# Two more planner gates on ScalarE copies in a kernel of a 2-D Fourier filter and a two-layer MLP

## The chip, the cores and the metric

The kernel runs on one core of a Trainium2 chip. The metric is the device time of one execution in microseconds (us); before the change the median of three runs is 149.49 us, from 149.27 to 149.67. TensorE (PE) multiplies matrices into PSUM, which has eight banks of 512 fp32 columns on 128 partitions. ScalarE (ACT) and VectorE (DVE) copy and compute on what lies in PSUM and in SBUF, GpSimd (POOL) and SyncE (SP) mostly issue DMAs here. Each engine works through its own instructions in order, and semaphores tie the engines together. In the profile, PEld is the weight load that goes ahead of a matmul.

## The reference

`x` is 2048 x 640, the hidden width is 1536, and all inputs are bf16.

```python
def _A_ref(x, w_r, w_i):
    X = jnp.fft.rfft2(x.astype(jnp.float32), axes=(-2, -1))
    X = X * (w_r + 1j * w_i)
    return jnp.fft.irfft2(X, s=(S, D), axes=(-2, -1)).astype(jnp.bfloat16)

def _B_ref(x, w1, b1, w2, b2):
    h = _gelu(jnp.einsum("bsd,df->bsf", x, w1) + b1)
    return jnp.einsum("bsf,fd->bsd", h, w2) + b2

xn = _layernorm(x, axis=-1)
return x + _A_ref(xn, A_w_r, A_w_i) + _B_ref(xn, B_w1, B_b1, B_w2, B_b2)
```

So each output row is the row of x, plus the filtered row, plus the row of the MLP, in which the vector b2 is the same for every row.

## The kernel before

**Tiles and stages.** The 2048 rows are 16 tiles of 128. Each is normalised (L667, DVE) and turned into `xnT`, the first eight tiles on PE, the last eight by transposing DMAs. The Fourier transforms are matmuls with tables. The forward one goes through PE groups that the code calls aps (one for each pair of tiles: ten matmuls of 128 columns with `gtab`; the DVE folds of L702 and L706 make their input, and a copy at L718 takes the 1280 columns of a pair out of PSUM into `XV`), bps, and cps; DVE multiplies by the filter (L833, L837); dps starts the way back, and after it sixteen transposing DMAs (L858, on SP) fill `XV` anew. The last part is the inverse transform of the rows, by the six `GROUPS` of two or three tiles, and then one closing matmul for each tile with `htab`, which goes into the same bank as the second MLP layer, is added to x + b2 by DVE (L950), and leaves for HBM.

**The MLP.** The first layer runs in five `BLOCKS` of 4, 2, 2, 4 and 4 tiles. In each block there are twelve hidden chunks; a chunk is five matmuls (for a block of four tiles, 512 columns each) into one bank, `hps`, and one activation on ScalarE (L760) that empties the bank into `gT`. The fourth block (number 3 in the code) is tiles 8 to 11. Its banks come from banks 4 to 7. The second layer of the tiles in `KEEP` is done early, in the middle of the kernel; its result sits in a pair of the same banks 4 to 7 (`kps`) until DVE adds it to x + b2 (L941). While such a pair is held, the block has two banks, and the third chunk of a block needs the bank of the first one back.

**b2's rows.** For each tile ScalarE writes the row b2 as fp32 to all 128 partitions (L917, 640 columns), into memory that the input x or `xnT` no longer needs; then a DMA from POOL (L935) adds x to it in place. Tile 11's row goes to the end of `X`, and needs the normalisation of all sixteen tiles to be done. The row has priority 5, the lowest of ScalarE's work.

**The inverse groups.** For each group, 8 or 12 matmuls with 128 rows and as many with 32 rows (with `getab`) write four banks (`eps`), of the banks 0 to 3. The 32-row ones read a remainder of `XV`; for groups 1 to 5 (`NEAR`) that remainder is first copied, 128 columns a tile, into `W1` (the remainder copies, L878, buffers xr1 to xr5, by ScalarE or DVE). All five can start when the last transposing DMA has landed. Two copies (L885, buffer yo), one for each half of the columns, then take the group out of PSUM; these are the inverse copies. DVE folds them twice (L889, L894) for the closing matmul.

**The planner.** Nothing of this order is written out by hand except where a gate says so. Every piece of work is a `K.op` with the engines that may do it and a cost for each, a priority, and what it reads and writes. `schedule` (L223) is a greedy list scheduler with its own clock: it always places the work that can start first; among what can start within 0.03 us of that on an engine, the highest priority goes first, and work that two engines may do goes to the one that would end it first. The order that comes out is the order of the instructions on each engine. `deps` (from reads, writes and `after`) become semaphore waits in `sync`. A `gate` does not: it only makes the planner place a piece no earlier, on its clock, than the start of the piece that it names. The costs that the change touches are these:

```python
def mm_us(n):
    return max(n / 2400.0 + 0.0027, 0.0265)
def dve_us(n, rate=1.0):
    return 0.066 + n / 960.0 / rate
def act_us(n, ptr=0):
    return 0.067 + n / 1200.0 + 0.078 * ptr
```

Of the kernel before, what the change touches and what calls it, by code (L numbers as in the profile page):

```python
# [9 lines left out]
ACT = mybir.ActivationFunctionType  # L10
# [3 lines left out]
D = 640  # L14
# [76 lines left out]
# [10 lines that stand above are left out]
# [78 lines left out]
class Sched:  # L179
# [190 lines left out]
    def emit(self, es, last):  # L370
# [54 lines left out]
CP = (((0, 1, ((0, 1, ["dve"]),)), (1, 3, ((1, 3, ["dve"]),)), (3, 5, ((3, 5, ["act"]),))), ((0, 2, ((0, 2, ["dve"]),)), (2, 5, ((2, 5, ["dve", "act"]),))),  # L425
      ((0, 2, ((0, 2, ["dve"]),)), (2, 5, ((2, 5, ["act", "dve"]),))), ((0, 2, ((0, 2, ["dve"]),)), (2, 5, ((2, 5, ["act", "dve"]),))))
NEAR = (1, 2, 3, 4, 5)
RP = 1.0
EARLY = 3
FIRST = ([(j, (c,), 0, 6) for c, j in ((0, 0), (0, 1), (0, 2), (1, 0), (1, 1), (1, 2), (0, 3), (1, 3))] + [(4, (0, 1), 0, 6)]  # L430
# [3 lines left out]
def bass_parallel_sum__spectral_gfnet__dense_activation_gelu__prompt_kernel(  # L434
# [20 lines left out]
    K = Sched(nc, ["sp", "pe", "act", "dve", "pool"])  # L455
    with ExitStack() as es:
        def sb(name, shape, dtype=BF):
            return es.enter_context(nc.sbuf_tensor(name, shape, dtype))

        def view(t, off, dims):  # L460
            width = int(np.prod(t.shape[1:]))
            return bass.AP(tensor=t, offset=off, ap=[[width, 128]] + dims)
# [15 lines left out]
        b2bc = sb("b2bc", [128, D])  # L478
# [23 lines left out]
        def psb(slot, dims, off=0, p0=0, n=128):  # L502
            return bass.AP(tensor=PS, offset=p0 * 4096 + slot * 512 + off, ap=[[4096, n]] + dims)
# [15 lines left out]
        def pe(segs, prio, lst, **kw):  # L519

            return K.op([("pe", sum(u for _, u in segs))], prio, mms(lst), alts=[segs], **kw)

        def copy(dst, src, scale=1.0):
            def f(e, name):
                if name == "act":
                    return e.activation(dst(), src(), ACT.Copy, scale=scale)  # L526
                return e.tensor_copy(dst(), src())  # L527
            return f
# [12 lines left out]
        for k in range(12):  # L541
# [3 lines left out]
             reads=[B_warm], writes=[B_id])  # L545
# [7 lines left out]
        B_b1, B_b2b, B_bz = Buf("b1t"), Buf("b2"), Buf("b1z")  # L553
# [76 lines left out]
        for c0, n in [(c, 1) for c in range(4)] + [(c, 2) for c in range(4, 16, 2)]:  # L630
            pr = 100 - c0 / 2
            B_mv, B_r = Buf("mv"), Buf("r")
            for c in range(c0, c0 + n):
                B_st = Buf("st")
                for h in range(2):
                    o = K.op([("dve", 0.393)], pr, lambda e, _, c=c, h=h: e.bn_stats(stats[:, c, 6 * h:6 * h + 6], view(X, c * D + H2 * h, [[1, H2]])),  # L636
                         reads=[B_x[c]], writes=[B_st], gate=mv_ops[:1])
# [4 lines left out]
                 reads=[B_mv, B_mh], writes=[B_r] + B_rs[a:b])  # L642

        for pair in range(8):
# [10 lines left out]
            for n in range(2):  # L655
                c = 2 * pair + n
                pr = 100 - c / 2
                cuts = [(0, 1), (1, 5)] if not c else [(0, 5)]
                B_xn = {}
                for j0, j1 in cuts:  # L660
# [4 lines left out]
                    if c == 0 and j0:  # L665
# [3 lines left out]
                        reads=[B_x[c], B_rs[c]], writes=[xn, b], gate=mv_ops[1:2] if c or j0 else [])  # L669
# [5 lines left out]
                if c in BYDMA:  # L675
                    ring_ops.append(K.op([("sp", 1.3)], 500, lambda e, _, c=c, n=n, xnv=xnv: e.dma_start_transpose(xnT[:, c, :, :], xnv(n, 0, [[1, D]])),
                         reads=[B_xn[0], xn], writes=[B_xnT[c]], rows=(40, 256)))
# [4 lines left out]
                for j0, j1, parts in CP[c] if c < 4 else ((0, 5, ((0, 5, ["dve", "act"]),)),):  # L682
# [11 lines left out]
                    for a, b, engs in parts:  # L694
# [4 lines left out]
                             reads=[tps], writes=[B_xnT[c]] if c > 3 else [B_xnT[c]] + [B_xnj[c, j] for j in range(a, b)])  # L699
            pr = 100 - pair - FOLD[pair]  # L700
# [3 lines left out]
            for k, op in enumerate((ALU.add, ALU.subtract)):  # L704
                for o_, o0, o1, w in ((128 * k, 0, H2 - 1, 128), (512 + 32 * k, 128, H2 - 129, 32)):
                    ring_ops.append(K.op([("dve", dve_us(4 * w, 2))], pr, lambda e, _, op=op, x1v=x1v, xfv=xfv, o_=o_, o0=o0, o1=o1, w=w: e.tensor_tensor(  # L706
                        out=xfv(o_, [[D, 2], [2 * w, 2], [1, w]]), in0=x1v(o0, [[D, 2], [H2, 2], [1, w]]), in1=x1v(o1, [[D, 2], [H2, 2], [-1, w]]), op=op),
                        reads=[x1], writes=[xf]))
            aps = Buf(f"aps{pair}", psum, 3, ZONE["aps"])
            for n in range(2):  # L710
                c = 2 * pair + n
                o = pe([("128", 5 * mm_us(128))], pr, lambda c=c, n=n, xfv=xfv, aps=aps: [
                    (psb(aps.slot, [[4, 64], [1, 2]], 256 * j + 2 * n), xfv(n * D + 128 * j, [[1, 128]]), gtab[:, 128 * c:128 * c + 128], True, True) for j in range(5)],
                    reads=[xf, B_g], writes=[aps])
                ring_ops.append(o)
                a_ops.append(o)
            for js in [[int(j) for j in g] for g in XASPLIT[pair].split()]:
# [3 lines left out]
                     reads=[aps], writes=[B_xa[pair]])  # L721

        B_gT = {}
        l1_ops, l1_of = [], {}
        h0 = [Buf(f"h0_{k}", psum, 1, ZONE["h0"]) for k in range(6)]
        first = {}

# [17 lines left out]
        for bi, (c0, nt) in enumerate(BLOCKS):  # L745
            for fc in range(NFC):
                hps = Buf(f"hps{bi}_{fc}", psum, 1, ZONE["hps"] if bi else ZONE["h1"]) if bi or fc > 5 else h0[fc]
                bg = Buf(f"gT{bi}_{fc}")
                for c in range(c0, c0 + nt):
                    B_gT[c, fc] = bg  # L750
                pr = PRIO["hps"] - bi - fc / 20
                part_ = []
                if bi or fc > 5:
                    for js in ((0, 1, 2), (3, 4)):
                        part_ = [pe([("128", len(js) * mm_us(128 * nt))], pr + 0.01 * len(part_), lambda c0=c0, nt=nt, fc=fc, hps=hps, js=js: [
                            (psb(hps.slot, [[1, 128 * nt]]), view(W1, F * j + 128 * fc, [[1, 128]]), xnT[:, c0:c0 + nt, j, :], j == 0, j == 4) for j in js],
                            reads=[B_w1s[fc // 6, j] for j in js] + B_xnT[c0:c0 + nt], writes=[hps], gate=part_)]
                        l1_ops += part_
                        l1_of.setdefault(bi, []).extend(part_)
                g_op = K.op([("act", act_us(128 * nt, 1))], pr + PRIO["gelu"] + GP[bi], lambda e, _, c0=c0, nt=nt, fc=fc, hps=hps: e.activation(  # L760
                    gT[:, fc, 128 * c0:128 * (c0 + nt)], psb(hps.slot, [[1, 128 * nt]]), ACT.Gelu_apprx_tanh, bias=b1col[:, fc:fc + 1], scale=1.0),
                    reads=[hps, B_b1c], writes=[bg])
                if not bi and fc == GATE0:
                    a_ops[0].gate.append(g_op)
                    a_ops[1].gate.append(g_op)
# [14 lines left out]
        def five_segs(n, t):  # L780
            return [("128", 4 * n * mm_us(Q4)), ("32", t)]

        pb_ops, filt_ops, d_ops, v_ops = [], [], [], []
        B_v = [Buf(f"v{q}") for q in range(16)]
        B_xb = {}
        xb_at = {}
        for gi, (c0, n) in enumerate(GROUPS):
# [4 lines left out]
                reads=B_xa + [B_e], writes=[bps, xb]))  # L792
# [8 lines left out]
        for P in range(4):  # L801
# [4 lines left out]
            for r in range(2):  # L806
# [6 lines left out]
                    reads=in_xb + [B_xbpad, B_m], writes=[cps])  # L813
# [16 lines left out]
            for pair, Y, TB, Z in zip(two, Ys, TBs, Zs):  # L830
                pr = PRIO["filt"] - pair / 5
                for k in range(2):
                    filt_ops.append(K.op([("dve", dve_us(4 * KP, 2))], pr, lambda e, _, k=k, Y=Y, TB=TB, pair=pair: e.tensor_tensor(  # L833
                        out=view(TT, TB.slot * 8 * KP + k * 4 * KP, [[2 * KP, 2], [KP, 2], [1, KP]]), in0=yv(Y, k == 1), in1=wv(pair, k), op=ALU.mult),
                        reads=[Y, B_wpad] + (B_w if pair == 7 else [B_w[k]]), writes=[TB], after=ring_ops))
# [4 lines left out]
            for v in range(2):  # L840
# [7 lines left out]
                for pp, U in enumerate(Us):  # L848
                    def evac(e, name, U=U, v=v, uv=uv, dps=dps, pp=pp):
                        for o_, w in ((0, 128), (512, 32)):  # L850
# [3 lines left out]
                         reads=[dps], writes=[U, B_us[pp]], after=a_ops + ring_ops)  # L854
# [13 lines left out]
            return [fin_ops[k[-AHEAD]]] if len(k) >= AHEAD else [l1_ops[-1]]  # L868
        B_yf = {}
        yf_at = {}  # L870
        for gi, (c0, n) in enumerate(GROUPS):
            yo, y2, yf = Buf(f"yo{gi}", p_yo), Buf(f"y2{gi}", p_y2), Buf(f"yf{gi}", p_yf)
            pr = PRIO["eps"] - c0 / 10
            eps_ = Buf(f"eps{gi}", psum, 4, ZONE["eps"])
            near = gi in NEAR
            B_xr = Buf(f"xr{gi}")
            if near:
                K.op([("act", act_us(128 * n)), ("dve", dve_us(128 * n))], pr + RP, copy(  # L878
                    lambda c0=c0, n=n: view(W1, REM + 128 * c0, [[128, n], [1, 128]]), lambda c0=c0, n=n: view(XV, 2048 * 4 + c0, [[1, n], [16, 128]])),
                     reads=B_v, writes=[B_xr], after=l1_ops)  # L880
            pe(five_segs(n, 0.071 * n + (0.014 if near else 0.059)), pr, lambda c0=c0, n=n, eps_=eps_, near=near: five(
                eps_.slot, n, lambda i, g, p0, k: part(W1, p0, k, REM + 128 * (c0 + i), [[1, 128]]) if near and g == 4 else part(XV, p0, k, 2048 * g + c0 + i, [[16, 128]]), getab),
                reads=B_v + [B_ge] + ([B_xr] if near else []), writes=[eps_], gate=[fin_ops[c0 - 5]] if c0 > 8 else [])
            for v in range(2):
                K.op([("act", act_us(320 * n)), ("dve", dve_us(320 * n))], pr,  # L885
                     copy(lambda v=v, yo=yo, n=n: view(Wf, YO + yo.slot * 3 * D + H2 * v, [[D, n], [Q4, 2], [1, Q4]]),
                          lambda v=v, eps_=eps_, n=n: psb(eps_.slot + 2 * v, [[Q4, n], [512, 2], [1, Q4]])), reads=[eps_], writes=[yo], after=filt_ops)
            for k, op in enumerate((ALU.add, ALU.subtract)):
                K.op([("dve", dve_us(320 * n, 2))], pr + 2, lambda e, _, k=k, op=op, yo=yo, y2=y2, n=n: e.tensor_tensor(  # L889
                    out=view(Wf, Y2 + y2.slot * 3 * D + (H2 - 1) * k, [[H2, 2 * n], [1 - 2 * k, Q4]]),  # L890
                    in0=view(Wf, YO + yo.slot * 3 * D, [[H2, 2 * n], [1, Q4]]), in1=view(Wf, YO + yo.slot * 3 * D + Q4, [[H2, 2 * n], [1, Q4]]), op=op),
                    reads=[yo], writes=[y2])
            for k, op in enumerate((ALU.add, ALU.subtract)):
# [3 lines left out]
                    reads=[y2], writes=[yf])  # L897
            for i in range(n):
                c = c0 + i
                kept = c in KEEP  # L900
                xo, os_ = Buf(f"xo{c}"), Buf(f"os{c}", p_os)
                if c in HOME:
                    ki = HOME.index(c)
                    free = [o for j, (t0, nt) in enumerate(BLOCKS) if t0 < 2 * ki + 2 for o in l1_of[j]]

                    def xov(o0, w, ki=ki):
                        return xnT[:].rearrange("p c j t -> p (c j t)").bitcast(F32)[:, D * ki + o0:D * ki + o0 + w]
                else:
                    ki = [b for b in range(16) if b not in HOME].index(c)
                    free = norm_ops[:2 * ki + 2]  # L910
# [3 lines left out]

                xb2 = Buf(f"xz{c}")
                if True:
                    K.op([("act", act_us(D))], 5, lambda e, _, xov=xov: e.activation(xov(0, D), b2bc[:], ACT.Copy), reads=[B_b2b], writes=[xb2], after=free, late=30.0)  # L917

                def sums(o0, w):

# [4 lines left out]
                def second(c, fps, o0, w, pr, gate, base=base):  # L925
                    part_ = []
                    for f0 in range(0, NFC, 3):
# [6 lines left out]
                pr = PRIO["fin"] - c / 10  # L934
                xo_ops[c] = K.op([("pool", 0.9)], 51 - c / 20, lambda e, _, c=c, xov=xov: e.dma_start(xov(0, D), xv[:, c, :], accum_op=ALU.add),  # L935
                     reads=[xb2], writes=[xo], rows=(8, "acc"))
# [6 lines left out]
                for o0, w in [(0, D)] if c < 15 else [(0, H2), (H2, Q4), (H2 + Q4, Q4)]:  # L943
# [5 lines left out]
                        reads=[yf, B_h], writes=[fps, B_f], gate=part_ + ([l1_ops[-1]] if kept else []))  # L949
# [4 lines left out]
                                     reads=[os_, B_o], rows=(8, w * 2 if w * 2 in ROW_NS else 1280)))  # L954
# [38 lines left out]
```

## Time and profile before

| | before |
|---|---|
| time, median of three runs | 149.49 us (149.27 to 149.67) |
| the profiled execution: time | 149.6 us |
| the profiled execution: span | 147.8 us |
| PE busy | 143.7 us, 97% of the span |
| DVE busy | 113.1 us, 77% |
| ACT busy | 83.7 us, 57% |
| POOL busy | 23.0 us, 16% |
| granted TensorE clock, mean | 1.000 |

The span goes from the first to the last instruction; the 1.8 us more of the time lie around it. Matmuls, copies and loads are issued by helpers, so their rows carry the helpers' lines: L515 every matmul, L526 a copy on ScalarE, L527 a copy on DVE, L510 a plain load. A line of the timeline gives start and duration in us, engine, source line, operation, output and input, form, and how many like instructions were merged (x); in brackets, how long the engine had been idle before and what ended that. A merged line's duration goes from the first start to the last end, and successive instructions of one engine overlap in part, so the start of the next line can lie before the end of this one. A matmul's end is modelled, and a matmul that waits for nothing starts before the one ahead of it has ended. A table of windows gives, for each stretch, the busy time of each engine and the number of instructions.

### The profile page before, as it was taken

Reading aid. Unit: us, or ns where it says so; the run is one execution under the profiler, and the core shown is the slowest. Engines: PE = TensorE matmul, PEld = TensorE weight load, DVE = VectorE, ACT = ScalarE, POOL = GpSimd, SP = SyncE. Lnnn points to the kernel's source line nnn. Section 1 sums busy time; section 2 is a strip of 40 time slices with the busy share of each in tenths; the row PEclk is TensorE's granted clock in tenths of the full one; section 3 lists DMA queues with packets and bytes.
Section 4 is the critical chain, followed back from the end, with each engine's and each line's share of the span. In section 5 each row is a group of like instructions: output and inputs, shape, how many; then the busy total and the mean of one; then the engine's idle time right before and its main releaser. Section 6 shows DMA issues by size and latency. Waiting matters only on the chain.

```text
span 147.8 us, 4165 instructions
## 1 busy us (share of the span) xinstructions
PE 143.7 (97%) x1754; PEld 89.5 (61%) x1754; DVE 113.1 (77%) x239; ACT 83.7 (57%) x143; POOL 23.0 (16%) x50
## 2 busy tenths in 40 slices
PE   7999999999999999999999999999999999999993
PEld 7889568898645554656455455334456666566572
DVE  2968999999999254979655796496206999999991
ACT  3123997899998875442878273697757324010300
POOL 4320111420000299600000000000006300000000
PEclk9999999999999999999999999999999999999999
DMA  4999999999688979994015206515453941232233
GB/s 127 291 315 401 360 246 232 362 209 118 122 151 155 239 176 256 268 267 111 0 32 114 40 4 120 60 23 117 84 117 72 225 131 44 99 129 89 89 135 92
DMA packets 28995, 23.00 MB, mean 156 GB/s; under 512 B 17840, under 2 KB 25776, under 8 KB 28848
## 3 DMA queue, kind: packets, MB, share of 16 engines
q1 hardware_dynamic: 26640, 17.48, 47.6%
q0 software_dynamic: 2336, 5.25, 15.5%
q8 instruction: 14, 0.23, 0.6%
q14 instruction: 5, 0.04, 0.1%
HBM read 13.54 MB, written 2.62 MB: 109 GB/s over the span
## 4 chain that ended last, share of the span: by engine, by line
PE 75%; ACT 12%; DMA 5%; SPq 4%; DVE 1%; issue 1%
PE ps L515 74%; ACT gT L760 4%; DMA W<-in_B_w_dram 4%; ACT X L917 3%; SPq L510 2%; SPq L858 2%; DMA XV<-U 2%; ACT xnT L917 2%; ACT W L526 2%; PE ps L687 1%; ACT XV L526 1%; DVE xnT L941 1%; ACT Wf L526 0%; DVE Wf L889 0%; DVE W L950 0%
## 5 line engine op out<-in xcount | busy, mean ns | idle before, releaser
L515 PE MATMUL ps<-W,gT 128*128 128x512 bf16 (+3 forms) x396 | 57.8, 295 | 0.1
L515 PE MATMUL ps<-xnT,W 128*128 128x512 bf16 (+2 forms) x384 | 57.4, 300 | 0.3
L515 PEld LDWEIGHTS ps<-W,gT 128*128 128x128 bf16 x396 | 29.9, 98 | 23.1 <-issue 1.9
L515 PEld LDWEIGHTS ps<-xnT,W 128*128 128x128 bf16 x384 | 31.6, 98 | 18.2 <-issue 2.0
L760 ACT ACTIVATE gT<-ps,b1col 128x512 bf16<-128x512 f32 (+1 forms) x60 | 35.1, 618 | 5.5 <-PE ps L515 4.6
L935 POOL DMA_DIRECT2D xnT<-in_A_x_dram x8 | 9.9, 2787 | 50.5 <-DMA XV<-U 50.5
L526 ACT ACTIVATE Wf<-ps 128x960 bf16<-128x960 f32 (+1 forms) x8 | 6.7, 867 | 17.9 <-PE ps L515 17.9
L636 DVE BATCH_NORM_STATS2 stats<-X 128x6 f32<-128x320 bf16 x32 | 13.7, 465 | 2.0 <-DMA X<-in_A_x_dram 2.0
L526 ACT ACTIVATE Xb<-ps 128x960 bf16<-128x960 f32 (+1 forms) x8 | 9.0, 1166 | 6.9 <-PE ps L515 6.8
L833 DVE TENSOR_TENSOR T<-Y,Wf 128x1288 bf16<-128x1288 bf16 x16 | 12.4, 823 | 0.0
L526 ACT ACTIVATE Y<-ps 128x644 bf16<-128x644 f32 x9 | 6.3, 707 | 7.5 <-PE ps L515 7.5
L935 POOL DMA_DIRECT2D X<-in_A_x_dram x8 | 7.2, 2076 | 20.3 <-DMA Wf<-in_A_w_i_dram 20.3
L941 DVE TENSOR_TENSOR X<-ps,X 128x640 f32<-128x640 f32 x8 | 6.6, 820 | 5.0 <-PE ps L515 5.0
L641 POOL TENSOR_TENSOR rstd<-mv,mhalf 128x2 f32<-128x2 f32 (+1 forms) x10 | 6.6, 663 | 21.0 <-DVE mv L639 21.0
L706 DVE TENSOR_TENSOR T<-T 128x512 bf16<-128x512 bf16 (+1 forms) x32 | 8.3, 314 | 0.1
L527 DVE CAST Xb<-ps 128x640 bf16<-128x640 f32 (+1 forms) x4 | 4.3, 1066 | 5.1 <-PE ps L515 5.1
L950 DVE TENSOR_TENSOR W<-ps,xnT 128x640 bf16<-128x640 f32 (+2 forms) x10 | 6.9, 685 | 1.1 <-PE ps L515 1.0
L527 DVE CAST Y<-ps 128x644 bf16<-128x644 f32 x7 | 5.8, 822 | 2.5 <-PE ps L515 2.5
L837 DVE TENSOR_TENSOR Z<-T 128x644 bf16<-128x644 bf16 x16 | 7.0, 486 | 0.8 <-PE ps L515 0.8
L526 ACT ACTIVATE XV<-ps 128x256 bf16<-128x256 f32 (+4 forms) x9 | 6.7, 750 | 1.3 <-PE ps L515 1.3
L889 DVE TENSOR_TENSOR Wf<-Wf 128x960 bf16<-128x960 bf16 (+1 forms) x12 | 6.8, 594 | 0.6 <-ACT Wf L526 0.6
L515 PE MATMUL ps<-etab,XV 32*128 32x160 bf16 (+1 forms) x128 | 7.2, 232 | 0.0
(59 smaller groups left out, 145.9 us busy)
## 6 DMA issues: line engine op xcount, KB each, us to landing
X<-in_A_x_dram POOLq DMA_DIRECT2D x8, 320.0 KB, 6.8
xnT<-in_A_x_dram POOLq DMA_DIRECT2D x8, 320.0 KB, 9.2
out_dram<-W SPq DMA_DIRECT2D x15, 160.0 KB, 1.8
X<-in_A_x_dram SPq DMA_DIRECT2D x6, 320.0 KB, 7.9
W<-in_B_w_dram SPq DMA_DIRECT2D x4, 480.0 KB, 10.4
W<-in_B_w_dram SPq DMA_DIRECT2D x6, 192.0 KB, 3.9
Wf<-in_A_w_r_dram SPq DMA_DIRECT2D x7, 160.5 KB, 9.4
Wf<-in_A_w_i_dram SPq DMA_DIRECT2D x7, 160.5 KB, 9.5
```

The lines of the kernel that those rows point to most:

```text
L515: ins = e.matmul(o_, lhsT=lw, rhs=rh, start=st, stop=sp_, skip_group_check=True)
L526: return e.activation(dst(), src(), ACT.Copy, scale=scale)
L527: return e.tensor_copy(dst(), src())
L636: o = K.op([("dve", 0.393)], pr, lambda e, _, c=c, h=h: e.bn_stats(stats[:, c, 6 * h:6 * h + 6], view(X, c * D + H2 * h, [[1, H2]])), read ...
L706: ring_ops.append(K.op([("dve", dve_us(4 * w, 2))], pr, lambda e, _, op=op, x1v=x1v, xfv=xfv, o_=o_, o0=o0, o1=o1, w=w: e.tensor_tensor(ou ...
L760: g_op = K.op([("act", act_us(128 * nt, 1))], pr + PRIO["gelu"] + GP[bi], lambda e, _, c0=c0, nt=nt, fc=fc, hps=hps: e.activation(gT[:, fc ...
L833: filt_ops.append(K.op([("dve", dve_us(4 * KP, 2))], pr, lambda e, _, k=k, Y=Y, TB=TB, pair=pair: e.tensor_tensor(out=view(TT, TB.slot * 8 ...
L837: K.op([("dve", dve_us(2 * KP, 2))], pr, lambda e, _, TB=TB, Z=Z, r=r, op=op: e.tensor_tensor(out=view(Zb, Z.slot * 4 * KP + r * KP, [[2 * ...
L917: K.op([("act", act_us(D))], 5, lambda e, _, xov=xov: e.activation(xov(0, D), b2bc[:], ACT.Copy), reads=[B_b2b], writes=[xb2], after=free, ...
L935: xo_ops[c] = K.op([("pool", 0.9)], 51 - c / 20, lambda e, _, c=c, xov=xov: e.dma_start(xov(0, D), xv[:, c, :], accum_op=ALU.add), reads=[ ...
L941: kept_ops.append(K.op([("dve", dve_us(D))], 30, lambda e, _, kps=kps, xov=xov: e.tensor_tensor(out=xov(0, D), in0=psb(kps.slot, [[1, D]]) ...
L950: K.op([("dve", dve_us(w))], 95, lambda e, _, os_=os_, fps=fps, o0=o0, w=w, xov=xov, base=base: e.tensor_tensor(out=view(W1, OST + os_.slo ...
```

## The change

Two gates are added. The second activation of the fourth block (`g31[1]`; `g31` collects the activations of block 3) becomes the gate of tile 11's b2 row. The two inverse copies of group 0 (`yo_ops`) become the gate of the remainder copy of group 5, which is the last of the five. No piece of work is added or removed.

```diff
 NEAR = (1, 2, 3, 4, 5)
+NEARG = 5
+LATEXZ = (11,)
+GX = 1
...
-        l1_ops, l1_of = [], {}
+        l1_ops, l1_of, g31 = [], {}, []
...
                     reads=[hps, B_b1c], writes=[bg])
+                if bi == 3:
+                    g31.append(g_op)
...
         yf_at = {}
+        yo_ops = []
         for gi, (c0, n) in enumerate(GROUPS):
...
-                     reads=B_v, writes=[B_xr], after=l1_ops)
+                     reads=B_v, writes=[B_xr], after=l1_ops, gate=yo_ops if gi >= NEARG else [])
...
             for v in range(2):
-                K.op([("act", act_us(320 * n)), ("dve", dve_us(320 * n))], pr,
+                yo1 = K.op([("act", act_us(320 * n)), ("dve", dve_us(320 * n))], pr,
...
+                if not gi:
+                    yo_ops.append(yo1)
...
                 xb2 = Buf(f"xz{c}")
                 if True:
-                    K.op([("act", act_us(D))], 5, lambda e, _, xov=xov: e.activation(xov(0, D), b2bc[:], ACT.Copy), reads=[B_b2b], writes=[xb2], after=free, late=30.0)
+                    K.op([("act", act_us(D))], 5, lambda e, _, xov=xov: e.activation(xov(0, D), b2bc[:], ACT.Copy), reads=[B_b2b], writes=[xb2], after=free, late=30.0, gate=[g31[GX]] if c in LATEXZ else [])
```

## The prediction

> **What bounds the kernel.** I read the engines' shares first, then the chain of waits, then a table of windows over the parts of the span, then the timelines of the two places that the change touches.
>
> ```profile
> span 147.8 us, 4165 instructions
> PE 143.7 (97%) x1754; PEld 89.5 (61%) x1754; DVE 113.1 (77%) x239; ACT 83.7 (57%) x143; POOL 23.0 (16%) x50
> PE 75%; ACT 12%; DMA 5%; SPq 4%; DVE 1%; issue 1%
> ...
> 42.00:44.00 2.00, 1.88 (x10) 0.68 (x9) 1.97 (x6) 2.00 (x4) 0.00 (x0) 1.00 1.02 169
> 44.00:112.00 68.00, 68.00 (x980) 34.81 (x979) 42.66 (x74) 43.36 (x72) 10.81 (x12) 1.00 0.57 121
> 112.00:118.00 6.00, 5.86 (x68) 3.82 (x66) 5.54 (x9) 3.72 (x5) 3.58 (x4) 1.00 0.74 159
> 118.00:145.00 27.00, 27.00 (x265) 17.35 (x264) 25.98 (x41) 5.07 (x6) 0.00 (x0) 1.00 0.31 100
> ```
>
> PE is the bound. From 42 us on its first column of busy time equals the window, except in two windows, and these are where the two pieces lie that the change moves. So a stall taken out there should come out at the end, unless PE meets it again, and nothing else that moves can gain anything.
>
> **First place: the third chunk of the fourth block.**
>
> ```profile
> 41.06 3.26 PE L515 MATMUL ps<-xnT,W 128*128 128x512 bf16 x13
> 44.16 0.72 PE L515 MATMUL ps<-gtab,T 128*128 128x128 bf16 x10
> 46.31 0.72 PE L515 MATMUL ps<-gtab,T 128*128 128x128 bf16 x10
> 46.86 1.89 PE L515 MATMUL ps<-xnT,W 128*128 128x512 bf16 x8
> 48.59 0.72 PE L515 MATMUL ps<-gtab,T 128*128 128x128 bf16 x10
> ...
> 43.50 0.33 PEld L515 LDWEIGHTS ps<-xnT,W 128*128 128x128 bf16 x3 [0.61 <-ACT gT L760]
> ...
> 41.40 0.85 ACT L917 ACTIVATE xnT<-b2bc 128x640 f32<-128x640 bf16 x1
> 42.02 0.85 ACT L917 ACTIVATE X<-b2bc 128x640 f32<-128x640 bf16 x1
> 42.65 0.80 ACT L760 ACTIVATE gT<-ps,b1col 128x512 bf16<-128x512 f32 x1
> 43.42 0.69 ACT L760 ACTIVATE gT<-ps,b1col 128x512 bf16<-128x512 f32 x1
> 44.92 1.24 ACT L526 ACTIVATE XV<-ps 128x1280 bf16<-128x1280 f32 x1 [0.81 <-PE ps L515]
> ```
>
> A matmul of 512 columns that waits for nothing takes one step of (48.59 - 46.86) / 8 = 0.216 us. The thirteen from 41.06 are chunks 0 and 1 of the block and three of chunk 2; they should need 13 x 0.216 = 2.81, and took 44.16 - 41.06 = 3.10. The **0.29 us** lost are the wait in PEld's row: the weights of chunk 2 are held until the activation of chunk 0 has given its bank back, at 42.65 + 0.80 = 43.45; PE goes on 0.06 later.
>
> That activation is late because two b2 rows stand before it. The one at 42.02 into `X`, the last of the eight there, is tile 11's. Chunk 0's last matmul starts at 41.06 + 4 x 0.216 = 41.92 and lasts 0.38, so ends at 42.30 (ScalarE starts some 0.04 after such an end: 44.16 + 0.72 = 44.88 against 44.92). Without the row the activation starts at 42.34, as the row before ends at 41.40 + 0.85 = 42.25; it takes 0.69 when it starts on an empty engine, like the second, and ends at 43.03. PE wants chunk 2 at 41.06 + 10 x 0.216 = 43.22, and gets it with 0.13 to spare. The stall is gone, all 0.29 of it.
>
> *What is late next* are the ten matmuls at 44.16, now wanted at 43.87. They need four folds of DVE, which nothing here moves:
>
> ```profile
> 42.83 1.02 DVE L706 TENSOR_TENSOR T<-T 128x512 bf16<-128x512 bf16 x4
> 44.81 1.03 DVE L706 TENSOR_TENSOR T<-T 128x512 bf16<-128x512 bf16 x4
> 41.42 1.48 DVE L527 CAST XV<-ps 128x1280 bf16<-128x1280 f32 x1
> ```
>
> The folds end at 43.85. From DVE's end to PE takes 0.06 (115.59 + 0.82 to 116.46, further down), from ScalarE's end 0.15 at 46.31 (after 44.92 + 1.24 = 46.16): so PE goes on at 43.91 or, at worst, 44.00. The gain is 0.25 or 0.17. I take 0.25, since the wait is for DVE; bounds 0 (below) to 0.29.
>
> *Where the row goes.* On the planner's clock chunk 1's activation begins when its matmuls are out; then come three matmuls of 512 columns and ten of 128, 3 x 0.216 + 10 x 0.056 = 1.208, before the copy of 1280 columns can begin. The activation takes 0.572 of it, the row 0.600: it fits with 0.036 left, ahead of the copy, and it starts before anything else that ScalarE could. The same on the chip: the second activation still starts at 43.42 (its matmuls, chunk 1, do not move) and ends at 44.11; the row adds 0.62 (from 41.40 to 42.02 between two of them), so ends near 44.73. The copy wants to start at 44.92 - 0.25 = 44.67, and an instruction here starts 0.2 before the end of the one ahead (42.02 against 42.25). It is not held. The 0.81 idle before 44.92 is the cover: without it the row would cost its 0.62. The next PE group (46.31) needs that copy, moved by 0.25 too, and the folds that end at 45.84, which is early enough for 46.06.
>
> ```profile
> 50.78 7.20 POOL L935 DMA_DIRECT2D X<-in_A_x_dram  x8 [20.28 <-DMA Wf<-in_A_w_i_dram]
> 55.22 0.81 DVE L941 TENSOR_TENSOR X<-ps,X 128x640 f32<-128x640 f32 x1
> 58.27 1.80 PE L515 MATMUL ps<-W,gT 128*128 128x512 bf16 x12
> ```
>
> Behind the row waits the DMA that adds x for tile 11, the last of these eight; POOL starts the first at 50.78, 6 us after the row's new end, so that costs nothing, and neither SP nor POOL is passed by anything. The kept tile's add at 55.22 hangs on the DMA and does not move; it ends at 56.03, and PE's next matmuls into its banks start at 58.27, so the lead of 0.25 survives it.
>
> **Second place: the first inverse group.**
>
> ```profile
> 111.85 2.31 ACT L526 ACTIVATE W<-XV 128x384 bf16<-128x384 bf16 x3 [2.19 <-DMA XV<-U]
> 112.72 0.88 ACT L526 ACTIVATE W<-XV 128x384 bf16<-128x384 bf16 x1
> 114.06 0.69 ACT L526 ACTIVATE Wf<-ps 128x640 bf16<-128x640 f32 x1
> 116.38 0.97 ACT L526 ACTIVATE Wf<-ps 128x960 bf16<-128x960 f32 x1 [1.64 <-PE ps L515]
> 113.49 0.82 DVE L527 CAST Wf<-ps 128x640 bf16<-128x640 f32 x1
> 114.78 0.89 DVE L889 TENSOR_TENSOR Wf<-Wf 128x640 bf16<-128x640 bf16 x2 [0.46 <-ACT Wf L526]
> 115.59 0.82 DVE L941 TENSOR_TENSOR xnT<-ps,xnT 128x640 f32<-128x640 f32 x1
> 113.37 1.80 PE L515 MATMUL ps<-W,gT 128*128 128x512 bf16 x12
> 115.94 0.39 PE L515 MATMUL ps<-getab,W 32*128 32x160 bf16 x12
> 116.46 0.99 PE L515 MATMUL ps<-W,gT 128*128 128x512 bf16 x6
> 119.31 0.39 PE L515 MATMUL ps<-getab,W 32*128 32x160 bf16 x12
> 119.63 0.45 PE L515 MATMUL ps<-Wf,htab 128*128 128x512 bf16 x2
> 136.99 0.32 PE L515 MATMUL ps<-getab,W 32*128 32x160 bf16 x8
> ```
>
> Three remainder copies run on ScalarE from 111.85; the first inverse copy follows at 114.06. Its other half ran on DVE from 113.49 to 114.31, then DVE sat 0.46 idle for ScalarE's half. DVE's folds, and then the kept tile's add at 115.59, come late by as much, and PE waits for that add: after the twelve 32-row matmuls it goes on 0.52 later (115.94 to 116.46), 0.32 where nothing holds it (119.31 to 119.63). Lost: **0.20**.
>
> With the gate the planner places the group-5 copy behind both inverse copies, on ScalarE, where it ends first; it is a swap of neighbours. The second remainder copy ends at 112.72 + 0.88 = 113.60; the inverse copy adds 0.59 (114.06 + 0.69 = 114.75 less the 114.16 at which the third copy ends) and ends at 114.19. DVE's half, ending at 114.31, is now the later one: DVE goes on at 114.35, 0.43 sooner. The add then waits for PE's twelve matmuls (113.37 + 1.80 = 115.17), ends at 116.0, and frees PE at 116.06, where PE wants 116.26. I take the whole 0.20; bounds 0 and 0.20. The moved copy runs from 114.2 to 114.8, in ScalarE's idle 1.64 before 116.38; its reader, group 5, comes at 136.99. DVE keeps 0.2 of lead over PE after it.
>
> **The sum.** 0.25 + 0.20 = 0.45; the profiled execution's 149.6 (147.8 of span and 1.8 around it) becomes 149.15. That run lies 0.11 above the median of 149.49, so the median becomes **149.04**.
>
> The Trainium skill (Perfetto Trace Analysis, Identifying the Most-Contended Engine) warns that TensorE's busy time is a poor measure because matmuls are pipelined. The windows agree: idle time alone, 2.00 - 1.88 and 6.00 - 5.86, would give 0.26 and a median of 149.23, where the starts give 0.49.
>
> **The rivals.** *Only one place pays.* If the row is still in the way at 44.7, or DVE's wake-up costs PE more, the first gain is lost again at 46.31; only 0.20 is left, 149.29. For it speaks that ScalarE is full from 30 to 44; against it the 0.81 idle. The same size comes if the second place pays nothing: 149.24.
>
> *Nothing.* Some DMA paces what follows (the last transposes land at 111.8, ended by "DMA XV<-U" in the row of ScalarE): 149.49. Against it, PE has no idle time from 44 to 112.
>
> *More.* DVE was 26.0 of 27 us busy from 118 to 145. If its lead of 0.43 and not PE's 0.20 is what counts there, the sum is 0.68: 148.81. Against it, PE is never idle there.
>
> *Slower.* The copy of 1280 columns may go to either engine, whichever ends it first. If the planner's ScalarE came out later than I have it (it has 1.134 for the copy against 1.399 on DVE, so from about 0.27 late on), the copy goes to DVE, where it takes 1.48 (41.42), ahead of the folds at 44.81; these end at 47.32, and PE goes on at 47.38 for 46.31. That is 1.07 lost, less 0.20 for the second place: 150.36. Against it: the row fits, if only by 0.036.
>
> **How the numbers follow.** About 0.3%, 0.45 us, is what a measurement of this kernel can tell from no change. Forecast 0.64; it lies on that mark, and I give 0.42 to beyond, because the first place has up to 0.04 more in it and the lead on DVE can only help, and 0.22 to short of it. More: 0.10. One place: 0.13, within the mark. Nothing: 0.04, within. Slower: 0.09. Faster 0.52, same 0.39, slower 0.09. The range holds the forecast, one place only, and most of "more", with the spread of the three runs: 148.75 to 149.45; the forecast's own is 148.95 to 149.15.
>
> **What would show it.** ScalarE: the row into `X` between the two activations and the copy of 1280 columns, and no wait of PEld on "gT L760" near 43. PE: the ten 128-column matmuls at about 43.9, and every later PE row 0.25 sooner up to 112. Behind the first inverse copy the shortest remainder copy; DVE's idle 0.46 before its L889 near zero; 0.32 between the 32-row matmuls and what follows, and then 0.45 to the end. It is wrong if an engine's order differs in more than these two swaps, if the 128-column group stays at 44.16, or if the later rows lose the lead again.

## The result and the profile after

| | before | after |
|---|---|---|
| time, median | 149.35 us (149.27 to 149.67) | 148.91 us (148.67 to 149.02) |
| runs | 6 | 6 |
| profiled execution: time, span | 149.6, 147.8 us | 148.91, 147.0 us |

The ratio is 0.9963, with a 95% interval of 0.995 to 0.9976. The medians lie 0.44 us apart; 0.45 was forecast. The forecast time itself, 149.04, was counted down from 149.49, the median of three runs; three more runs have put the median of before at 149.35. Two executions of the experiments, one of 242.54 us at a granted clock of 0.566 (`after_again`) and one of 290.99 us at 1.0 (`copy_on_dve`), were in a slow state and count in no ratio.

The code after the change has a few lines more, so helpers have new numbers: L518 is every matmul (L515 before), L529 a copy on ScalarE, L530 a copy on DVE, L763 the MLP's activations, L925 b2's rows, L709 the folds (L706), L897 the first folds of the inverse groups (L889), L949 the kept tile's add (L941). Instruction for instruction the order of PE, DVE, POOL and SP is the old one; on ScalarE two pieces have moved, tile 11's row and the remainder copy of group 5. (Some matmul records are missing in this trace; the second trace of the changed kernel, `after_again`, has all 1754, in the old order.)

First the chain of waits, which follows the work that ended last back in time. Three pieces of it before, from the first place (start, duration, what; left out is 0.04 of issue):

```profile
42.25 0.62 ACT X L917
42.87 0.59 ACT gT L760
...
43.51 62.03 PE ps L515 x888
```

and after, the pieces that cover the first place and the second:

```profile
36.22 17.40 PE ps L518 x158
...
113.15 5.90 PE ps L518 x73
```

Before, the chain left PE at 43.51 and went back through the activation and tile 11's row on ScalarE. After, it passes 42 to 44 and 115 to 117 on PE alone.

The timeline of PE after the change, at the two places and at the end (start, duration, line, operation, form, count):

```profile
40.93 2.97 PE L518 MATMUL ps<-xnT,W 128*128 128x512 bf16 x13
43.76 0.73 PE L518 MATMUL ps<-gtab,T 128*128 128x128 bf16 x10
44.33 1.67 PE L518 MATMUL ps<-xnT,W 128*128 128x512 bf16 x7
45.91 0.72 PE L518 MATMUL ps<-gtab,T 128*128 128x128 bf16 x10
...
115.50 0.39 PE L518 MATMUL ps<-getab,W 32*128 32x160 bf16 x12
115.82 0.99 PE L518 MATMUL ps<-W,gT 128*128 128x512 bf16 x6
...
144.41 0.23 PE L518 MATMUL ps<-Wf,htab 128*128 128x160 bf16 x1
```

and two lines of before beside it, the last matmul, and the weight load behind the 32-row matmuls at the second place, which waits for the kept tile's add:

```profile
145.09 0.23 PE L515 MATMUL ps<-Wf,htab 128*128 128x160 bf16 x1
...
116.46 0.66 PEld L515 LDWEIGHTS ps<-W,gT 128*128 128x128 bf16 x6 [0.33 <-DVE xnT L941]
```

Against the rows of before, PE is ahead by 0.13 already at 40.93 (41.06 before). That is not the change, since nothing that moved lies earlier; executions differ by that much in their start. The thirteen matmuls of the first place took 43.76 - 40.93 = 2.83 instead of 3.10: 0.27 saved, and the lead is 0.40 at 43.76 and at 45.91, and 0.44 at 115.50. The wait behind the 32-row matmuls took 0.32 instead of 0.52: 0.20 saved, and the lead is 0.64 at 115.82 and 0.68 at the last matmul. So of the 0.68 by which these two executions differ on PE at the end, 0.13 came before the change could act, 0.27 and 0.20 at the two places, and 0.08 in small pieces between and behind them.

The timeline of ScalarE after, at both places:

```profile
42.21 0.69 ACT L763 ACTIVATE gT<-ps,b1col 128x512 bf16<-128x512 f32 x1
43.29 0.69 ACT L763 ACTIVATE gT<-ps,b1col 128x512 bf16<-128x512 f32 x1 [0.39 <-PE ps L518]
43.87 0.73 ACT L925 ACTIVATE X<-b2bc 128x640 f32<-128x640 bf16 x1
44.53 1.24 ACT L529 ACTIVATE XV<-ps 128x1280 bf16<-128x1280 f32 x1
...
113.05 0.70 ACT L529 ACTIVATE Wf<-ps 128x640 bf16<-128x640 f32 x1
113.64 0.66 ACT L529 ACTIVATE W<-XV 128x256 bf16<-128x256 bf16 x1
```

The row into `X` now fills the idle time ahead of the copy of 1280 columns (the 0.81 of before is gone), and the shortest remainder copy stands behind the first inverse copy. DVE, which moved with them, in its own timeline:

```profile
42.69 1.02 DVE L709 TENSOR_TENSOR T<-T 128x512 bf16<-128x512 bf16 x4
...
113.97 0.89 DVE L897 TENSOR_TENSOR Wf<-Wf 128x640 bf16<-128x640 bf16 x2
114.78 0.82 DVE L949 TENSOR_TENSOR xnT<-ps,xnT 128x640 f32<-128x640 f32 x1
```

The folds of the first place end at 43.71, and PE's ten matmuls follow at 43.76. At the second place the 0.46 of idle time before the first fold is gone. The weight loads of the first place show what is left to wait for:

```profile
42.95 0.46 PEld L518 LDWEIGHTS ps<-xnT,W 128*128 128x128 bf16 x3 [0.19 <-ACT gT L763]
43.76 0.56 PEld L518 LDWEIGHTS ps<-gtab,T 128*128 128x128 bf16 x10 [0.36 <-DVE T L709]
```

The load for chunk 2 still waits for the activation, 0.19 where before it waited 0.61. The prediction's sign was that this wait would be gone. It costs PE nothing, because loads run ahead of the matmuls: the load starts at 42.95, and PE wants chunk 2 at 40.93 + 10 x 0.216 = 43.09. The next load waits for the folds, and that is the wait PE meets now: 0.02, as the thirteen take 2.83 where 13 x 0.216 are 2.81.

One view misleads here. In the table of windows, from 44 to 112 (window, its length, then busy time and count of PE, PEld, DVE, ACT, POOL, and clock, DMA share, GB/s):

```profile
44.00:112.00 68.00, 67.05 (x971) 34.76 (x979) 42.96 (x74) 44.25 (x72) 11.14 (x13) 1.00 0.56 119
```

PE seems to have become 0.95 us idler. But it has 971 matmul records for 979 weight loads, where before had 980 for 979: records are missing, not work (`after_again`, the same kernel, has 980 there and 68.00 us of PE). The starts above are what can be compared.

### The profile page after: what moved, and what is told of

Its sections match the earlier page's. It is cut to its first block, busy times and chain, and to the rows that moved or that the text cites. A ratio compares the mean times of both kernels' runs of the same rounds, so it can differ in the third digit from the quotient of the medians.

```text
span 147.0 us, 4149 instructions
## 1 busy us (share of the span) xinstructions
PE 141.9 (97%) x1738; PEld 89.8 (61%) x1754; DVE 113.3 (77%) x239; ACT 83.8 (57%) x143; POOL 23.0 (16%) x50
## 4 chain that ended last, share of the span: by engine, by line
PE 93%; DVE 2%; DMA 2%; issue 1%
PE ps L518 92%; PE ps L690 2%; DMA X<-in_A_x_dram 2%; DVE stats L639 1%; DVE U L670 0%; DVE mv L642 0%; DVE W L958 0%
## 5 line engine op out<-in xcount | busy, mean ns | idle before, releaser
L518 PE MATMUL ps<-xnT,W 128*128 128x512 bf16 (+2 forms) x384 | 57.1, 300 | 0.0
L518 PE MATMUL ps<-W,gT 128*128 128x512 bf16 (+3 forms) x382 | 55.5, 292 | 1.4 <-issue 0.9
L518 PEld LDWEIGHTS ps<-W,gT 128*128 128x128 bf16 x396 | 29.9, 98 | 22.9 <-issue 1.9
L518 PEld LDWEIGHTS ps<-xnT,W 128*128 128x128 bf16 x384 | 31.8, 98 | 17.5 <-issue 2.0
L763 ACT ACTIVATE gT<-ps,b1col 128x512 bf16<-128x512 f32 (+1 forms) x60 | 35.0, 616 | 6.1 <-PE ps L518 5.1
L529 ACT ACTIVATE Wf<-ps 128x960 bf16<-128x960 f32 (+1 forms) x8 | 6.7, 869 | 17.6 <-PE ps L518 17.6
L529 ACT ACTIVATE Xb<-ps 128x960 bf16<-128x960 f32 (+1 forms) x8 | 9.1, 1169 | 6.9 <-PE ps L518 6.7
L529 ACT ACTIVATE Y<-ps 128x644 bf16<-128x644 f32 x9 | 6.3, 707 | 7.5 <-PE ps L518 7.5
L949 DVE TENSOR_TENSOR X<-ps,X 128x640 f32<-128x640 f32 x8 | 6.5, 819 | 5.0 <-PE ps L518 5.0
L709 DVE TENSOR_TENSOR T<-T 128x512 bf16<-128x512 bf16 (+1 forms) x32 | 8.3, 314 | 0.1
L530 DVE CAST Xb<-ps 128x640 bf16<-128x640 f32 (+1 forms) x4 | 4.3, 1067 | 5.1 <-PE ps L518 5.1
L530 DVE CAST Y<-ps 128x644 bf16<-128x644 f32 x7 | 5.8, 822 | 2.4 <-PE ps L518 2.4
L518 PE MATMUL ps<-etab,XV 32*128 32x160 bf16 (+1 forms) x128 | 7.2, 232 | 0.0
L529 ACT ACTIVATE XV<-ps 128x256 bf16<-128x256 f32 (+4 forms) x9 | 6.8, 751 | 0.5 <-PE ps L518 0.5
L897 DVE TENSOR_TENSOR Wf<-Wf 128x960 bf16<-128x960 bf16 (+1 forms) x12 | 6.8, 593 | 0.3 <-ACT Wf L529 0.2
```

The source lines that it names most:

```text
L518: ins = e.matmul(o_, lhsT=lw, rhs=rh, start=st, stop=sp_, skip_group_check=True)
```

## The experiments

All kernels but one are the changed kernel with one edit; times are medians, ratios are against the kernel before on the same chip, which had a median of 149.34 beside `row_only`, `copy_only`, `long_row_before` and `long_row_after`, and of 149.39 beside the others. The short measure used throughout is a duration on PE between two starts, so a late or early start of the whole execution drops out: at the first place the thirteen matmuls (before 3.10, after 2.83), at the second the twelve 32-row matmuls (before 0.52, after 0.32).

### Each place alone

`row_only` keeps the gate of tile 11's row and drops the other:

```diff
-NEARG = 5
+NEARG = 6
```

> Only the gate on tile 11's b2 row. Theory (each place pays for itself, PE carries the lead to the end): PE 0.25 us earlier from the ten 128-column matmuls at 43.9 on, no further step at 116, the wait behind the 32-row matmuls of group 1 still 0.52 instead of 0.32; time 149.35 - 0.25 = 149.10, ratio 0.9983. Rival (all of the gain comes from the closing stage, where DVE leads): no lead at the end, ratio 1.000. Rival (all of it comes from the first place): 148.91, ratio 0.997.

Measured: 149.04 us, ratio 0.9978 (0.9967 to 0.999), the median 0.30 us below that of before. PE's timeline:

```profile
40.84 2.97 PE L518 MATMUL ps<-xnT,W 128*128 128x512 bf16 x13
43.69 0.73 PE L518 MATMUL ps<-gtab,T 128*128 128x128 bf16 x10
...
115.45 0.39 PE L518 MATMUL ps<-getab,W 32*128 32x160 bf16 x12
115.94 0.99 PE L518 MATMUL ps<-W,gT 128*128 128x512 bf16 x6
```

The first place takes 2.85, as in the changed kernel; the second takes 0.49, nearly as before. So the first gain is there without the second gate, and it lasts to the end.

`copy_only` keeps only the gate of the remainder copy:

```diff
-LATEXZ = (11,)
+LATEXZ = ()
```

> Only the gate on the group-5 remainder copy. Theory: the stall at 43 stays (0.29 lost), PE is 0.20 earlier from 116 on; time 149.35 - 0.20 = 149.15, ratio 0.9987. Rival (the lead of 0.43 on DVE counts in the closing stage and not PE's 0.20): 148.92, ratio 0.997. Rival (no gain): 1.000.

Measured: 149.33 us, from 148.95 to 150.17, ratio 0.9998 (0.9981 to 1.0015). By itself this says that the second place pays nothing. The profiled execution, of 150.06 us, shows what else there was, 100 us ahead of the second place, and the second place itself:

```profile
16.64 0.72 PE L518 MATMUL ps<-gtab,T 128*128 128x128 bf16 x10 [0.29 <-DMA gtab<-c_G]
...
116.60 0.39 PE L518 MATMUL ps<-getab,W 32*128 32x160 bf16 x12
116.92 0.93 PE L518 MATMUL ps<-W,gT 128*128 128x512 bf16 x5
```

PE waited for a table that landed late, in a part that the edit does not touch; at the second place it took 0.32, as in the changed kernel. The lowest time of this kernel, 148.95, is 0.17 below the lowest of before beside it, 149.12. That late starts raised the other high times too is likely but not shown, since only one execution was profiled. The same kernel was run again as `copy_only_again`:

> The kernel with only the gate on the group-5 remainder copy, once more, because its first measurement came out at 0.9998 with an interval from 0.998 to 1.0015, and its profiled execution began with a table that landed late (PE waits 0.29 for gtab at 16.6). Theory (the second place pays 0.20, the first measurement was spread by the start): 149.34 - 0.20 = 149.14, ratio 0.9987, lowest time below that of before. Rival (the second place pays nothing in the end): 149.34, ratio 1.000.

Measured: 149.11 us, from 148.92 to 149.27, ratio 0.9971 (0.9956 to 0.9986), the median 0.28 us below that of before, the lowest time 0.22 below (148.92 against 149.14). Its PE:

```profile
40.98 3.25 PE L518 MATMUL ps<-xnT,W 128*128 128x512 bf16 x13
44.07 0.72 PE L518 MATMUL ps<-gtab,T 128*128 128x128 bf16 x10
...
115.83 0.39 PE L518 MATMUL ps<-getab,W 32*128 32x160 bf16 x12
116.15 0.99 PE L518 MATMUL ps<-W,gT 128*128 128x512 bf16 x6
```

3.09 at the first place, as before; 0.32 at the second, as after. Each gate acts on its own place and on no other, and except for the first measurement of `copy_only` the intervals leave out 1.000. So "only one place pays" and "nothing" fall.

"More", by which DVE's 0.43 at the second place counts, is not decided by the times: it asked for a ratio of 0.997, the theory for 0.9987, and 0.9971 was measured with an interval that ends just short of the theory. The rows decide it. DVE did gain most of the 0.43: in the changed kernel its first fold went from 114.78 to 113.97, by 0.81, and 0.44 of this is the lead that PE had at 115.50 already; 0.37 are left. But PE gained 0.20 there, and no more behind it: from where it goes on to its last matmul are 145.09 - 116.46 = 28.63 before, 144.41 - 115.82 = 28.59 after, and 28.59 in `copy_only_again` too. If DVE's lead counted in the closing stage, that stretch would be shorter by some 0.2; it is shorter by 0.04.

The changed kernel itself, run once more beside these:

> The changed kernel as it is, on the chip and in the rounds of the others. Theory (both places add up): 148.89, ratio 0.997, 0.2 below the kernel with one gate on the row alone (149.04). Rival (the second place pays nothing): 149.04, ratio 0.998.

Measured: 148.78 us, ratio 0.9951 (0.9935 to 0.9968), the median 0.61 us below that of before; the thirteen matmuls took 2.84, the 32-row ones 0.31. The parts, 0.30 and 0.28 by the medians, add up to 0.58, so the two gains do not overlap. The lowest times of each kernel, which late starts raise least, say the same: 0.22 for the row alone, 0.17 and 0.22 for the copy alone, 0.48 for both (148.66 against 149.14).

### A longer row in the old place

If the row holds the activation, and the activation the bank, then a row twice as long must cost PE all of its second half. In the kernel *before*, and later in the changed one, tile 11's row is preceded by another of the same 640 columns, written to memory that nothing reads at that time. The planner does not know of it, so the order stays. The row's `K.op`, left out here, calls this function:

```diff
+        def row(e, xov, c):
+            if c == 11:
+                e.activation(Zb[:].bitcast(F32)[:, 0:D], b2bc[:], ACT.Copy)
+            return e.activation(xov(0, D), b2bc[:], ACT.Copy)
...
```

> The kernel before, with tile 11's row preceded by one more like it (640 columns of b2 written to memory that is unused then), in the same place ahead of the fourth block's first activation. Order otherwise that of before. Theory (the bank that chunk 2 waits for comes back as late as ScalarE's rows push the activation): the activation starts 0.62 later, at 43.27, the stall of PE grows from 0.29 to 0.91, all later PE rows are 0.62 late; time 149.35 + 0.62 = 149.97, ratio 1.0042. Rival (PE was about to wait for DVE's folds or a DMA anyway): less than 0.3 of it reaches the end, ratio below 1.002.

Measured: 149.91 us, ratio 1.004 (1.0025 to 1.0054), 0.57 longer. ScalarE, then PE:

```profile
41.81 0.85 ACT L868 ACTIVATE Z<-b2bc 128x640 f32<-128x640 bf16 x1
42.44 0.84 ACT L869 ACTIVATE X<-b2bc 128x640 f32<-128x640 bf16 x1
43.07 1.37 ACT L760 ACTIVATE gT<-ps,b1col 128x512 bf16<-128x512 f32 x2
```

```profile
40.87 2.32 PE L515 MATMUL ps<-xnT,W 128*128 128x512 bf16 x10
43.92 0.82 PE L515 MATMUL ps<-xnT,W 128*128 128x512 bf16 x3 [0.73 <-ACT gT L760]
44.58 0.72 PE L515 MATMUL ps<-gtab,T 128*128 128x128 bf16 x10
```

From 40.87 to 44.58 are 3.71, that is 0.61 more than before, for a row that adds 0.63 (41.81 to 42.44). PE's idle time now has its own entry, put down to the activation. The longer row's time comes out on PE one for one: what ScalarE runs ahead of that activation, PE pays.

### A longer row in the new place

The same edit in the changed kernel asks whether the 0.81 idle ahead of the copy was what hid the row.

> The changed kernel with the same second row of 640 columns beside tile 11's, now behind the second activation, ahead of the copy of 1280 columns. Theory (the 0.8 us in which ScalarE idles there is the cover, one row fits and two do not): the copy starts about 0.5 and ends 0.58 later than in the changed kernel, the next 128-column group of PE (45.9) and all behind it are 0.58 late; time 148.91 + 0.58 = 149.49, ratio 1.001 to before. Rival (ScalarE has room there for more, any row behind the activations is free): 148.91, ratio 0.997.

Measured: 149.44 us, ratio 1.0004 (0.999 to 1.0019): the whole gain of the change is lost again. ScalarE, then PE:

```profile
43.94 0.73 ACT L873 ACTIVATE Z<-b2bc 128x640 f32<-128x640 bf16 x1
44.57 0.72 ACT L874 ACTIVATE X<-b2bc 128x640 f32<-128x640 bf16 x1
45.19 1.23 ACT L529 ACTIVATE XV<-ps 128x1280 bf16<-128x1280 f32 x1
```

```profile
41.00 2.97 PE L518 MATMUL ps<-xnT,W 128*128 128x512 bf16 x13
43.83 0.73 PE L518 MATMUL ps<-gtab,T 128*128 128x128 bf16 x10
...
46.56 0.72 PE L518 MATMUL ps<-gtab,T 128*128 128x128 bf16 x10 [0.49 <-ACT XV L529]
```

The first place still takes 2.83. But the copy now starts behind the second row, and the ten matmuls that need it come 46.56 - 43.83 = 2.73 after the ten before them, where the changed kernel takes 45.91 - 43.76 = 2.15: 0.58 lost. One row fits in the idle time, a second doesn't.

### Other idle times for the row

Two more positions ask whether the place behind the second activation is special. `gate_first_activation` has `GX = 0`, `gate_fifth_activation` has `GX = 4`, which lands the row in ScalarE's next idle time.

> The changed kernel with tile 11's row behind the first instead of the second activation of the fourth block. Theory (only the first activation's end counts; the second's bank is wanted again only at 44.76 and the second ends at 44.1 at the latest): as the changed kernel, 148.9, ratio 0.997. Rival (the second activation is on the path too): 0.13 slower than the changed kernel, ratio 0.998.

> The changed kernel with tile 11's row behind the fifth activation of the fourth block, at 48.4, in the next idle time of ScalarE (0.52 ahead of a copy of 1024 columns at 48.95). Theory (the row needs any idle slot it fits in; here it overlaps the copy's start by 0.1 at most, which the overlap of successive instructions takes up): as the changed kernel within 0.1, 148.9 to 149.0, ratio 0.997. Rival (the slot at 43.9 is the only good one): the copy ends 0.1 or more later and the matmuls of the first forward group with it, 149.05 or more, ratio 0.998 or above.

Measured: 148.84 us, ratio 0.9958 (0.9942 to 0.9974), and 148.91 us, ratio 0.9969 (0.9951 to 0.9988); the thirteen matmuls take 2.83 and 2.82. In the first, the row delays the second activation, to 43.50, and that costs nothing: it ends at 44.18, and PE wants its bank only for chunk 3, at 44.33 + 2 x 0.216 = 44.76 by the changed kernel's rows. ScalarE of the first kernel:

```profile
42.88 0.73 ACT L925 ACTIVATE X<-b2bc 128x640 f32<-128x640 bf16 x1
43.50 0.68 ACT L763 ACTIVATE gT<-ps,b1col 128x512 bf16<-128x512 f32 x1
```

In the other, the row stands between an activation and the next pair's copy at 50.01:

```profile
49.39 0.73 ACT L925 ACTIVATE X<-b2bc 128x640 f32<-128x640 bf16 x1
50.01 1.02 ACT L529 ACTIVATE XV<-ps 128x1024 bf16<-128x1024 f32 x1
```

The copy at 50.01 starts 8.00 behind the thirteen matmuls (42.01, further down), in the changed kernel 8.02 (48.95, from 40.93), so it is not held. Both kernels take the changed kernel's time within the spread: the three places tried behind the first activation serve alike. In each of them ScalarE has idle time for the row before PE wants something back.

### The copy of 1280 columns on DVE

The "slower" rival was a copy that the planner sends to DVE. It did not happen, but its price can be tried: that one copy (pair 6) is allowed on DVE alone.

```diff
-                K.op([("dve", dve_us(256 * len(js))), ("act", act_us(256 * len(js)))], pr,
+                K.op([("dve", dve_us(256 * len(js)))] + ([("act", act_us(256 * len(js)))] if pair != 6 else []), pr,
```

> The changed kernel, with the copy of 1280 columns of the pair near 45 us allowed on DVE alone, as the 'slower' rival has it. The rival as it was priced (copy ends 47.32 by DVE's clock, PE loses 1.07 at the next ten 128-column matmuls): 148.9 + 1.07 = about 150.0. But the planner, which knows the copy's cost, then puts matmuls of the MLP ahead of those ten, so PE need not stand still; if its plan holds, the loss is the 0.15 by which the planner's own end is later: about 149.05, with PE's rows at 46 to 48 without a wait over 0.1. The two are told apart by the wait of PE behind the copy on DVE: about 1.07, or next to nothing.

Measured: 148.89 us, ratio 0.9963 (0.9949 to 0.9978). DVE, then PE:

```profile
44.45 1.48 DVE L530 CAST XV<-ps 128x1280 bf16<-128x1280 f32 x1
```

```profile
44.23 3.40 PE L518 MATMUL ps<-xnT,W 128*128 128x512 bf16 x15
47.47 0.72 PE L518 MATMUL ps<-gtab,T 128*128 128x128 bf16 x10
```

The copy takes the 1.48 of the rival's price. But PE has fifteen matmuls of the MLP there instead of seven: 47.47 - 44.23 = 3.24, which is 15 x 0.216. It waits for nothing. A planner that knows the copy's cost orders the other engines by it too; the price of 1.07 was that of a copy moved with all else in place.

## Why the prediction was right

**First place, 0.25 forecast, 0.27 measured (0.25 to 0.28 over the kernels with this gate).** Each step is in the rows. The activation was to start at 42.34 and end at 43.03; it starts at 42.21 and ends at 42.90, the same less the 0.13 of the start. The ten matmuls were to be late by the folds, at 43.91; they come at 43.76, which is 43.89 with the 0.13, 0.05 behind the folds (the working took 0.06, where its rows 116.41 and 116.46 give 0.05 too). One sign failed: the weight load of chunk 2 still waits 0.19 for the activation. The working compared PE's matmuls with the activation's end and left out that loads run ahead of them; the 0.13 to spare came out as 0.14 (43.09 less 42.95). The wake-up of 0.15 from ScalarE, which would have left 0.17, does not apply, since the wait is for DVE.

**Where the row goes.** It was to end near 44.73 and the copy to start at 44.67; less 0.13 that is 44.60 and 44.54, and they are at 43.87 + 0.73 = 44.60 and 44.53. The cover of 0.81 was named as what hides it, with 0.62 as the price without; `long_row_after` lost 0.58.

**Second place, 0.20 forecast, 0.20 measured (0.17 against `row_only`, which takes 0.49 there).** The inverse copy ends at 113.75; 114.19 was forecast, the same with PE's lead of 0.44 there. DVE's fold starts 0.06 later than forecast (113.97 against 114.35 less 0.44). Most of that came out of the lead that DVE was to keep: the add ends at 115.60, 0.22 ahead of 115.82, where 0.26 was forecast (116.0 against 116.26). PE's own 32-row matmuls end the gain at 0.20.

**The sum.** The rows give 0.27 + 0.20 = 0.47, the two pairs of medians 0.44 and 0.61, the parts run alone 0.58. The lowest times give 0.48. What the medians have above 0.47 is of the size by which medians of this kernel move with its start (149.33 and 149.11 for the same kernel), so it isn't assigned. That 0.44 came out so near to 0.45 is therefore in part luck: the interval of the ratio reaches from 0.36 to 0.75 us, and by it the 0.3% of the forecast may or may not have been passed. The median of 148.91 lies 0.13 under the forecast 149.04, just outside the forecast's own 148.95 to 149.15, because the median of before fell by 0.14 with three more runs.

PE's idle time alone gave 0.26 in the windows of before, little over half of what the starts gave and the runs confirmed; the windows of after would give a loss. By the Trainium skill (Perfetto Trace Analysis, Identifying the Most-Contended Engine) matmul busy time is not a good measure of how close TensorE is to its roofline, because pipelined matmuls look smaller in the trace. It was a poor measure here too, but for other reasons: a matmul's modelled end, 0.38 after its start where the step is 0.216, covers part of a wait (0.12 idle for 0.29 lost), and records were missing after.

**The rivals.** "Only one place" and "nothing" fell with the parts run alone, "more" by PE's rows to the end, not by the times. "Slower" did not occur: the planner's order has the two swaps and nothing else. Its price was wrong too: a copy on DVE was to cost PE 1.07, and a kernel with that copy on DVE takes 148.89, the changed kernel's time. So the 0.09 given to slower rested on a price that the planner would have spared. That the planner's order could have changed in another, dearer way was not tried.

## What to carry to other kernels

In this kernel PE is the bound, and the order on the engine that feeds it mattered only where PE wanted something back. For such a kernel: find the wait in the weight loads, look which low-priority piece stands ahead of its releaser, and look whether that engine is idle for as long as the piece takes somewhere behind it; both numbers can be read off the trace of before. The gain of such a move ends at whatever is late next, here DVE's folds (0.27 of 0.29) and PE's own matmuls (0.20 of DVE's 0.37), so cost that before the wait itself. And where a planner makes the order, price a rival as the planner would order it, not as one piece moved with all else in place.

## What was not expected of the hardware

Loads at the start sometimes land late: in two of the eleven profiled executions, `copy_only` and `gate_fifth_activation`, PE waited for the table `gtab`. Both kernels differ from the changed one only behind 40 us. The longer wait, in `gate_fifth_activation`, on PE, DVE and PE's weight loads:

```profile
16.79 0.72 PE L518 MATMUL ps<-gtab,T 128*128 128x128 bf16 x10 [0.44 <-DMA gtab<-c_G]
...
42.01 2.98 PE L518 MATMUL ps<-xnT,W 128*128 128x512 bf16 x13
...
15.36 1.28 DVE L639 BATCH_NORM_STATS2 stats<-X 128x6 f32<-128x320 bf16 x3 [1.11 <-DMA X<-in_A_x_dram]
...
21.69 0.28 PEld L690 LDWEIGHTS ps<-ident,T 128*128 128x128 bf16 x5 [0.50 <-DVE T L670]
```

At 42.01 PE is 1.08 behind the changed kernel's 40.93, more than its wait for the table, and this execution took 149.84 where the kernel's median is 148.91. The rest follows a load of `x` that landed late too: DVE stood idle 1.11 for it and started its statistics at 15.36 instead of the changed kernel's 14.24, and at 21.69 PE, 1.01 behind the changed kernel's 20.68 by then, waits for DVE's normalisation. `copy_only` shows the same, with 0.93 of idle time on DVE. Why the loads were late is open. The delay is larger than the whole effect of the change, which is why the experiments were read by durations between two rows of PE first and by times second.
